# A gated scan and two MLPs on one core: the first products of a slot split by PSUM bank, and their copy in two steps

## The chip, the cores and the metric

The kernel runs on one core of a Trainium2 chip. What is measured is the device time of one execution in microseconds (us). Engines are named as the profile names them: PE is TensorE's matmul, PEld its weight load, DVE VectorE, ACT ScalarE, POOL GpSimd, SP SyncE, whose queue issues the DMAs.

## The reference

Three stages run behind each other on 12160 tokens (2 sequences of 6080) with 256 features, all in float32:

```
sig = 1 / (1 + exp(-f_logit));  f = lower_bound + (1 - lower_bound) * sig
h_t = f_t * h_(t-1) + (1 - f_t) * x_t                    # gated scan over the sequence
y   = relu(h @ w_in1)**2 @ w_out1                        # MLP 0, 256 -> 2048 -> 256
z   = y @ w_in2;  out = where(z > 0, z, exp(min(z, 0)) - 1) @ w_out2   # MLP 1, ELU, 256 -> 2048 -> 256
```

## The kernel before

Tokens are cut into 25 blocks: 256, then 22 of 512, then 384, then 256. Each block goes through MLP 0 (m=0, behind the scan) and MLP 1 (m=1). The hidden width is cut into 8 groups g. One block with one group in one MLP is a *slot* (m, b, g); there are 400. The first four blocks of MLP 0 are "plain" (32 slots); the other 368 slots form their first product from seven smaller products that are combined afterwards, and the change touches these 368 alone. With a block of 512 tokens n is 256, half the block. Blocks are taken in pairs whose slots are woven together, first a pair in MLP 1, then a later pair in MLP 0, and so on: such a *round* of two pairs has 16 slots of m=1 and 16 of m=0, and the middle of the run is a row of equal rounds.

Every float32 number is carried as a high and a low part, so each product is three matmuls. In a slot of the 368:

- `first` (L600 through `products`): 9 matmuls into columns 1, 2 and 3 of a PSUM tile `pc` of four columns of n. A column of 256 float32 is 1 KB, so columns 0 and 1 lie in one 2 KB bank, 2 and 3 in the next. Two `pc` tiles rotate.
- `snap` (L628, ACT): one copy of columns 1 to 3 out to the tile `s`. It is called "the copy" below. `pair` (L631, DVE) adds two of its columns.
- `out` (L699): the second product of an earlier slot, from its `g` tile; 24 matmuls of 256 columns for m=1, 12 of 512 for m=0. In PE's order it mostly lies between `first` and `later`; in some slots near the two ends of the run nothing lies there.
- `later` (L600): 12 matmuls that add to columns 0 to 3 of the same `pc`. They change what the copy has to read before, so they come behind it.
- Then `common` (L636, DVE, reads column 0), `mid_blocks` (L643, DVE, columns 2 and 3), `last_block` (L639, DVE), `first_block` (L646, ACT, column 1), which write the tile `r`; for m=0 `relu` (L649) and `square` (L652) on ACT, for m=1 `below` (L656) and `exp` (L659) on ACT and `elu` (L662) on DVE; and `high_part` (L667, ACT) and `low_part` (L672, DVE), which make `g`.

The order of the work is made when the program is built. `pe_order` fixes PE's order. Every step is given to `Order` with an engine, an assumed duration, a due time and the keys that it reads and writes; `Order.run` plays the engines forward with these assumed numbers, takes on each engine the ready step with the earliest due time, and writes the instructions in the order in which the steps began in that plan. The keys serve the plan alone. Which semaphores an instruction waits for is worked out afterwards from the tiles that the written instructions touch. Each engine runs its instructions strictly in the written order. These lines give the steps that the change touches:

```
"first": ["PE", ... 4.5 * ROW * 2 * n, in_due[s], first, [*X[:2], ws], [pc, ("pe",)]],
"later": ["PE", 6 * ROW * 2 * n, mid_due[s], later, [*X, ws], [pc, ("pe",)]],
["ACT", act(3 * n, True), snap, [pc], [sk]],
["DVE", dve(n), common, [pc, sk], [(*sk, 0), rk]],
["ACT", act(n, True), first_block, [pc, rk], [r0]],
```

Of the kernel before, what the change touches and what calls it, by code (L numbers as in the profile page):

```python
# [15 lines left out]
P = 128  # L16
# [138 lines left out]
def kernel(  # L155
# [59 lines left out]


    NW, NX = 7, 7
    FIRST_PRODUCTS = ((0, 0, 1), (3, 1, 2), (5, 2, 3))
    LATER_PRODUCTS = ((2, 3, 1), (4, 5, 0), (6, 4, 2), (1, 6, 3))
    PLAIN_PRODUCTS = ((1, 0, 0), (3, 1, 0), (0, 0, 1), (2, 1, 1))  # L220

    def plain(m, b):
        return m == 0 and b < PLAIN
# [9 lines left out]
    def new(tag, shape, dtype=F32, name=None):  # L233
        return pools[tag].tile(shape, dtype, tag=name or tag, name=name or tag)
# [29 lines left out]
    for i, s in enumerate(slots + [None] * (LAG + 1)):  # L264
        n = sizes[s[1]] if s else 0
        if s:
            if s[0] == 1 and s[2] == 0:
                while any(p[:2] == (0, s[1]) for _, p, _ in pending):
                    _, p, _ = pending.pop(0)
                    pe_order.append(("out", p))  # L270
                    out_due[p] = now
                    now += 12 * ROW * sizes[p[1]]
            pe_order.append(("first", s))
            in_due[s] = now
            now += (12 if plain(*s[:2]) else 4.5) * ROW * n
        while pending and (not s or i - pending[0][0] >= LAG or now - pending[0][2] >= AGE * sizes[pending[0][1][1]] / TB):
            _, p, _ = pending.pop(0)
            pe_order.append(("out", p))
            out_due[p] = now
            now += 12 * ROW * sizes[p[1]]  # L280
        if s:
            pe_order.append(("later", s))
            mid_due[s] = now
            now += (0 if plain(*s[:2]) else 6) * ROW * n
            pending.append((i, s, now))
# [3 lines left out]
    def act(n, psum=False):  # L289
        return (0.05 if psum else 0.09) + n / 1172  # L290
# [300 lines left out]
    def add_slot(i, m, b, g, wk):  # L591
# [3 lines left out]
        tag = set_of[m, b]  # L595

        def products(which, ws):
            for w, v, c in which:
                for q, (p, r) in enumerate(((0, 0), (0, 1), (1, 0))):
                    nc.tensor.matmul(  # L600
                        t["pc"][:, c], lhsT=ws[:, p, w], rhs=x_t[m, b][:, r, v],
                        start=(which is FIRST_PRODUCTS and q == 0 and c in (1, 2)), stop=(q == 2),
                        skip_group_check=True,
                    )

        def first(e):
            t["pc"] = ph.tile([P, 4, HB], F32, tag="pc", name="pc")[:, :, :n]
            t["ws"] = ws = ws_t[m, g]
            if not plain(m, b):
                products(FIRST_PRODUCTS, ws)  # L610
                return
            for w, k, c in PLAIN_PRODUCTS:
                for q, (p, r) in enumerate(((0, 0), (0, 1), (1, 0))):
                    nc.tensor.matmul(  # L614
                        t["pc"][:, 2 * c : 2 * c + 2], lhsT=ws[:, p, w], rhs=x_t[m, b][:, r, 2 * k : 2 * k + 2],
                        start=(k == 0 and q == 0), stop=(k == 1 and q == 2),
                    )
# [2 lines left out]
            t["r"] = new("r", [P, 4 * HB])[:, : 4 * n]  # L620
            nc.scalar.activation(t["r"].rearrange("p (q i) -> p q i", q=4), t["pc"], AF.Relu)

        def later(e):
            products(LATER_PRODUCTS, t["ws"])

        def snap(e):
            t["s"] = new("s", [P, 3, HB])[:, :, :n]
            nc.scalar.activation(t["s"], t["pc"][:, 1:4], AF.Copy)  # L628

        def pair(e):  # L630
            nc.vector.tensor_tensor(t["s"][:, 1], t["s"][:, 1], t["s"][:, 2], op=ALU.add)  # L631
# [70 lines left out]
        if g == 0:  # L702
# [3 lines left out]
        accs = acc_k[m, b]  # L706
        X = [(*tag, k) for k in range(2 if plain(m, b) else 4)]
        pc, sk, rk, gk = (x + (i,) for x in (("pc",), ("s",), ("r",), ("g",)))
        sk = ("s", n_s[0])
        n_s[0] += not plain(m, b)  # L710
        ek = ("e", n_elu[0])
# [2 lines left out]
        r0, r1, r2, r3, r4 = ((*rk, k) for k in range(5))  # L714
        gh, gl = (*gk, 0), (*gk, 1)
        pe = {
            "first": ["PE", (12 if plain(m, b) else 4.5) * ROW * 2 * n, in_due[s], first, [*X[:2], ws], [pc, ("pe",)]],
            "later": ["PE", 6 * ROW * 2 * n, mid_due[s], later, [*X, ws], [pc, ("pe",)]],
            "out": ["PE", 12 * ROW * 2 * n, out_due[s], out_mm, [gh, gl, ("w", m, g)], [*accs, ("pe",)]],
        }  # L720
        N = 4 * n
        before = [
            ["ACT", act(3 * n, True), snap, [pc], [sk]],
            ["DVE", dve(n), pair, [sk], [(*sk, 1)]],
        ]
        after = [
            ["DVE", dve(n), common, [pc, sk], [(*sk, 0), rk]],
            ["DVE", dve(2 * n), mid_blocks, [pc, (*sk, 0), rk], [r1]],
            ["DVE", dve(n), last_block, [(*sk, 0), (*sk, 1), rk], [r2]],
            ["ACT", act(n, True), first_block, [pc, rk], [r0]],  # L730
        ]
        if plain(m, b):
            before = []
            after = [
                ["ACT", act(N, True), whole_relu, [pc], [rk]],
                ["ACT", act(N), square, [rk], [r4]],
            ]
        elif m == 0:
# [101 lines left out]
    for kind, s in pe_order:  # L840
# [11 lines left out]
        if kind != "later" or not plain(m, b):  # L852
            one = made[s][0][kind]
            order.add(one[0], one[1], one[2], *one[3:])
        if kind == "later":
            chain(out_due[s], made[s][2])
        if kind == "first":
            chain(mid_due[s], made[s][1])
        if kind == "out" and g == KG - 1:
            add_evacuation(m, b)  # L860
# [34 lines left out]
```

## Time and profile before

| | us |
|---|---|
| three runs | 2182.74, 2184.99, 2193.29 (median 2184.99) |
| the profiled execution | 2181.22 |
| its span, first to last instruction | 2179.4 |
| PE busy | 2085.8 (96%) |
| PEld busy | 1968.1 (90%) |
| DVE busy | 1729.9 (79%) |
| ACT busy | 1712.1 (79%) |

Busy time is the union of an engine's instructions, and the rest of the span is idle. An idle stretch is put down to the instruction whose semaphore ended it. The first matmul starts at 25.8 us and the plain slots end near 207 us; from about 410 to 1783 us the rounds follow each other at a pitch of some 172.3 us; behind that come the small last blocks. The granted TensorE clock is 9 tenths or more in each of the 40 slices of the page. In rows of the order, as the built program has it, a wait is shown in square brackets by the engine whose semaphore is waited for, and x11 stands for eleven equal instructions that follow each other.

### The profile page before, as it was taken

What the parts mean: (1) busy time and instruction counts of PE and PEld (TensorE: products, weight loads), DVE (VectorE), ACT (ScalarE), POOL (GpSimd) and SP (SyncE); (2) the same over time, 40 slices, a digit from 0 to 9 for tenths busy, and PEclk for the clock granted to TensorE, in tenths of its full rate; (3) what the DMA queues carried; (4) which work ended last, traced back from release to release, by engine and by line L of the source; (5) the groups of instructions that cost most, each with busy time, mean ns of one, the idle gap of its engine ahead of it and who ended that gap; (6) DMA issues with size and microseconds to landing.
All of it is one profiled execution on the core that took longest, in us unless ns stands there. A gap on an engine that the chain in (4) does not pass through costs nothing.

```text
span 2179.4 us, 38016 instructions
## 1 busy us (share of the span) xinstructions
PE 2085.8 (96%) x15072; PEld 1968.1 (90%) x15072; DVE 1729.9 (79%) x2938; ACT 1712.1 (79%) x2243; POOL 0.2 (0%) x4
## 2 busy tenths in 40 slices
PE   2999899999999999999999999999999999999998
PEld 1877889999999899899899899999999989999998
DVE  5787896986985986987887798798698598677675
ACT  3786787887887887888888888788788788778675
POOL 0000000000000000000000000000000000000000
PEclk9999999999999999999999999999999999999999
DMA  5777643432542442433433433343253243233524
GB/s 154 218 236 241 194 157 108 120 124 94 135 130 95 130 130 92 133 101 119 120 109 124 126 102 124 113 115 126 100 136 122 95 123 127 87 112 106 185 85 141
DMA packets 213049, 282.84 MB, mean 130 GB/s; under 512 B 111112, under 2 KB 137608, under 8 KB 212872
## 3 DMA queue, kind: packets, MB, share of 16 engines
q1 hardware_dynamic: 212872, 280.42, 41.2%
q8 instruction: 119, 1.95, 0.4%
q14 instruction: 58, 0.48, 0.1%
HBM read 236.59 MB, written 43.78 MB: 129 GB/s over the span
## 4 chain that ended last, share of the span: by engine, by line
PE 68%; DVE 19%; ACT 6%; DMA 4%; issue 2%; SPq 1%; DVEq 0%; ACTq 0%
PE acc L699 35%; PE pc L600 31%; DVE g L672 4%; DVE r L643 2%; DVE F L565 2%; PE pc L614 1%; DVE r L662 1%; DVE s L631 1%; ACT s L628 1%; DVE r L639 1%; DMA ws<-wd 1%; DVE s L636 1%; DMA xs<-in_x_dram 1%; DVE fT L548 1%; DVE xA L500 1%
## 5 line engine op out<-in xcount | busy, mean ns | idle before, releaser
L699 PE MATMUL acc<-wo,g 128*128 128x256 f32 x4560 | 585.1, 283 | 17.8 <-DVE g L672 16.7
L699 PEld LDWEIGHTS acc<-wo,g 128*128 128x128 f32 x4560 | 561.3, 189 | 23.2 <-DVE g L672 21.4
L699 PE MATMUL acc<-g,wo 128*128 128x512 f32 (+2 forms) x2400 | 555.9, 382 | 2.1 <-DVE wo L403 2.1
L600 PE MATMUL pc<-xB,ws 128*128 128x256 f32 (+2 forms) x3864 | 507.6, 281 | 11.7 <-ACT s L628 11.2
L600 PE MATMUL pc<-xA,ws 128*128 128x256 f32 (+2 forms) x3864 | 506.3, 280 | 12.9 <-ACT s L628 12.9
L600 PEld LDWEIGHTS pc<-xA,ws 128*128 128x128 f32 x3864 | 481.6, 189 | 24.2 <-ACT s L628 18.5
L672 DVE TENSOR_TENSOR g<-r,g 128x1024 fp32r<-128x1024 f32 (+2 forms) x400 | 465.6, 1164 | 45.0 <-ACT g L667 43.9
L600 PEld LDWEIGHTS pc<-xB,ws 128*128 128x128 f32 x3864 | 482.5, 189 | 20.4 <-ACT s L628 13.7
L699 PEld LDWEIGHTS acc<-g,wo 128*128 128x128 f32 x2400 | 427.8, 189 | 78.0 <-DVE wo L403 2.3
L667 ACT ACTIVATE g<-r 128x1024 fp32r<-128x1024 f32 (+2 forms) x400 | 406.3, 1016 | 58.0 <-DVE r L662 50.6
L636 DVE TENSOR_TENSOR s<-pc,s 128x256 f32<-128x256 f32 (+2 forms) x368 | 150.5, 409 | 286.8 <-PE pc L600 286.1
L628 ACT ACTIVATE s<-pc 128x768 f32<-128x768 f32 (+2 forms) x368 | 286.9, 780 | 62.4 <-PE pc L600 61.1
L643 DVE TENSOR_TENSOR r<-pc,s 128x512 f32<-128x512 f32 (+2 forms) x368 | 244.3, 664 | 11.3 <-ACT r L646 5.9
L662 DVE SCALAR_TENSOR_TENSOR r<-e,r 128x1024 f32<-128x1024 f32 (+1 forms) x200 | 232.3, 1162 | 25.2 <-ACT e L659 25.2
L646 ACT ACTIVATE r<-pc 128x256 f32<-128x256 f32 (+2 forms) x368 | 137.0, 372 | 139.2 <-DVE r L643 87.1
L656 ACT ACTIVATE e<-r 128x1024 f32<-128x1024 f32 (+1 forms) x200 | 202.8, 1014 | 19.3 <-DVE r L639 14.9
L649 ACT ACTIVATE r<-r 128x768 f32<-128x768 f32 (+2 forms) x168 | 138.5, 824 | 97.8 <-DVE r L639 97.7
L652 ACT ACTIVATE r<-r 128x1024 f32<-128x1024 f32 (+1 forms) x200 | 203.6, 1019 | 5.7
L659 ACT ACTIVATE e<-e 128x1024 f32<-128x1024 f32 (+1 forms) x200 | 203.2, 1016 | 5.1
L631 DVE TENSOR_TENSOR s<-s 128x256 f32<-128x256 f32 (+2 forms) x368 | 150.1, 408 | 16.8 <-ACT s L628 9.4
L639 DVE TENSOR_TENSOR r<-s 128x256 f32<-128x256 f32 (+2 forms) x368 | 149.5, 406 | 0.0
L614 PE MATMUL pc<-xA,ws 128*128 128x256 f32 (+1 forms) x192 | 41.0, 368 | 29.0 <-DVE xA L494 25.8
(49 smaller groups left out, 858.0 us busy)
## 6 DMA issues: line engine op xcount, KB each, us to landing
ws<-wd SPq DMA_DIRECT2D x192, 896.0 KB
out_dram<-o SPq DMA_DIRECT2D x47, 256.0 KB
fs<-in_f_logit_dram SPq DMA_DIRECT2D x176, 64.0 KB
xs<-in_x_dram SPq DMA_DIRECT2D x176, 64.0 KB
xd<-o SPq DMA_DIRECT2D x44, 256.0 KB
F<-xd SPq DMA_DIRECT2D x44, 256.0 KB
st<-in_moe_w_out_dram SPq DMA_DIRECT2D x16, 512.0 KB
wd<-wp SPq DMA_DIRECT2D x24, 256.0 KB
```

The costliest lines, as they stand in the source:

```text
L600: nc.tensor.matmul(t["pc"][:, c], lhsT=ws[:, p, w], rhs=x_t[m, b][:, r, v], start=(which is FIRST_PRODUCTS and q == 0 and c in (1, 2)), st ...
L628: nc.scalar.activation(t["s"], t["pc"][:, 1:4], AF.Copy)
L631: nc.vector.tensor_tensor(t["s"][:, 1], t["s"][:, 1], t["s"][:, 2], op=ALU.add)
L636: nc.vector.tensor_tensor(t["s"][:, 0], t["pc"][:, 0], t["s"][:, 0], op=ALU.add)
L643: nc.vector.tensor_tensor(t["c"][:, 1:3], t["pc"][:, 2:4], u, op=ALU.add)
L652: nc.scalar.activation(t["r"], t["r"], AF.Square)
L656: nc.scalar.activation(t["e"], t["r"], AF.Relu, scale=-1.0)
L659: nc.scalar.activation(t["e"], t["e"], AF.Exp, scale=-1.0)
L662: nc.vector.scalar_tensor_tensor(t["r"], t["e"], 1.0, t["r"], op0=ALU.subtract, op1=ALU.max)
L667: nc.scalar.activation(t["g"][:, 0], t["r"], AF.Copy)
L672: nc.vector.tensor_tensor(t["g"][:, 1], t["r"], t["g"][:, 0].bitcast(F32), op=ALU.subtract)
L699: nc.tensor.matmul(a, lhsT=u, rhs=v, start=clear and k == 0, stop=two and k == 2, skip_group_check=True)
```

## The change

The nine matmuls of `first` become two steps: three into column 1 (`first`, one bank) and six into columns 2 and 3 (`next`, the other bank), in the same order as before. The twelve of `later` become six into columns 0 and 1 (`later`) and six into columns 2 and 3 (`last`); here the order of the columns changes from 1, 0, 2, 3 to 0, 1, 2, 3. The copy becomes two copies, column 1 by itself and columns 2 and 3. In the planner's keys `pc` becomes two keys, p0 and p1, one for each bank; `first_block` and `common` now ask for p0 alone. The PSUM tile `pc` is still one tile of two banks. Lines of the changed kernel: products L608, copies L638, `pair` L642, `common` L647, `last_block` L650, `mid_blocks` L654, `first_block` L657, `relu` L660, `square` L663, `below` L667, `exp` L670, `elu` L673, `high_part` L678, `low_part` L683, `out` L710.

```diff
-    FIRST_PRODUCTS = ((0, 0, 1), (3, 1, 2), (5, 2, 3))
-    LATER_PRODUCTS = ((2, 3, 1), (4, 5, 0), (6, 4, 2), (1, 6, 3))
+    PRODUCTS = {
+        "first": ((0, 0, 1),), "next": ((3, 1, 2), (5, 2, 3)),
+        "later": ((4, 5, 0), (2, 3, 1)), "last": ((6, 4, 2), (1, 6, 3)),
+    }
...
             pe_order.append(("first", s))
             in_due[s] = now
             now += (12 if plain(*s[:2]) else 4.5) * ROW * n
+            if not plain(*s[:2]):
+                pe_order.append(("next", s))
...
             pe_order.append(("later", s))
+            if not plain(*s[:2]):
+                pe_order.append(("last", s))
...
-        def snap(e):
-            t["s"] = new("s", [P, 3, HB])[:, :, :n]
-            nc.scalar.activation(t["s"], t["pc"][:, 1:4], AF.Copy)
+        def snap(a, z):
+            def go(e):
+                if a == 1:
+                    t["s"] = new("s", [P, 3, HB])[:, :, :n]
+                nc.scalar.activation(t["s"][:, a - 1 : z - 1], t["pc"][:, a:z], AF.Copy)
+            return go
...
-            "first": ["PE", (12 if plain(m, b) else 4.5) * ROW * 2 * n, in_due[s], first, [*X[:2], ws], [pc, ("pe",)]],
-            "later": ["PE", 6 * ROW * 2 * n, mid_due[s], later, [*X, ws], [pc, ("pe",)]],
+            "first": ["PE", (12 if plain(m, b) else 1.5) * ROW * 2 * n, in_due[s], first, [*X[:2], ws], [p0, ("pe",)]],
+            "next": ["PE", 3 * ROW * 2 * n, in_due[s], more("next"), [*X[:2], ws], [p1, ("pe",)]],
+            "later": ["PE", 3 * ROW * 2 * n, mid_due[s], more("later"), [*X, ws], [p0, ("pe",)]],
+            "last": ["PE", 3 * ROW * 2 * n, mid_due[s], more("last"), [*X, ws], [p1, ("pe",)]],
...
-            ["ACT", act(3 * n, True), snap, [pc], [sk]],
-            ["DVE", dve(n), pair, [sk], [(*sk, 1)]],
+            ["ACT", act(n, True), snap(1, 2), [p0], [(*sk, 0)]],
+            ["ACT", act(2 * n, True), snap(2, 4), [p1, (*sk, 0)], [(*sk, 1)]],
+            ["DVE", dve(n), pair, [(*sk, 1)], [(*sk, 1)]],
...
-            ["DVE", dve(n), common, [pc, sk], [(*sk, 0), rk]],
-            ["DVE", dve(2 * n), mid_blocks, [pc, (*sk, 0), rk], [r1]],
+            ["DVE", dve(n), common, [p0], [(*sk, 0), rk]],
+            ["DVE", dve(2 * n), mid_blocks, [p1, (*sk, 0), rk], [r1]],
             ["DVE", dve(n), last_block, [(*sk, 0), (*sk, 1), rk], [r2]],
-            ["ACT", act(n, True), first_block, [pc, rk], [r0]],
+            ["ACT", act(n, True), first_block, [p0, rk], [r0]],
```

**Place 1: PE, near the end of the run, a slot with nothing between its first nine and its last twelve matmuls (block of 384, n = 192).** Before:

```order
L600 MATMUL pc<-xA,ws 128x192 [waits PE_49]
L600 MATMUL pc<-xA,ws 128x192 x8
L600 MATMUL pc<-xA,ws 128x192 [waits Activation_49]
L600 MATMUL pc<-xA,ws 128x192 x11
L600 MATMUL pc<-xA,ws 128x192 [waits DVE_49,PE_49]
L600 MATMUL pc<-xA,ws 128x192 x8
```

And now:

```order
L608 MATMUL pc<-xA,ws 128x192 [waits PE_49]
L608 MATMUL pc<-xA,ws 128x192 x8
L608 MATMUL pc<-xA,ws 128x192 [waits Activation_49]
L608 MATMUL pc<-xA,ws 128x192 x5
L608 MATMUL pc<-xA,ws 128x192 [waits Activation_49]
L608 MATMUL pc<-xA,ws 128x192 x5
L608 MATMUL pc<-xA,ws 128x192 [waits DVE_49,PE_49]
L608 MATMUL pc<-xA,ws 128x192 x8
```

The twelve matmuls had one wait for ACT, ahead of the first; here they have two, ahead of the first and the seventh. The built program has this second wait in 14 of the 368 slots.

**Place 2: ACT, m=0 slots in the middle of a round (s is the tile of the copy, r<-pc is `first_block`, 768 wide is `relu`, r<-r 1024 `square`, g `high_part`).** Before:

```order
L646 ACTIVATE r<-pc 128x256 [waits DVE_49,PE_49]
L628 ACTIVATE s<-pc 128x768 [waits PE_49]
L649 ACTIVATE r<-r 128x768 [waits DVE_49]
L652 ACTIVATE r<-r 128x1024 [waits Activation_49]
L667 ACTIVATE g<-r 128x1024 [waits Activation_49]
```

And now, two slots:

```order
L657 ACTIVATE r<-pc 128x256 [waits DVE_49]
L638 ACTIVATE s<-pc 128x256 [waits PE_49]
L660 ACTIVATE r<-r 128x768 [waits DVE_49]
L638 ACTIVATE s<-pc 128x512
L663 ACTIVATE r<-r 128x1024 [waits Activation_49]
L678 ACTIVATE g<-r 128x1024 [waits Activation_49]
L638 ACTIVATE s<-pc 128x256 [waits PE_49]
L657 ACTIVATE r<-pc 128x256 [waits DVE_49]
L638 ACTIVATE s<-pc 128x512
L660 ACTIVATE r<-r 128x768 [waits DVE_49]
L663 ACTIVATE r<-r 128x1024 [waits Activation_49]
L678 ACTIVATE g<-r 128x1024 [waits Activation_49]
```

The copy stood in one piece behind `first_block`; its second step now stands behind `relu` in one slot and behind `first_block` in the next, and has no wait of its own.

**Place 3: ACT, the change from m=0 to m=1 within a round.** Before:

```order
L628 ACTIVATE s<-pc 128x768 [waits PE_49]
L646 ACTIVATE r<-pc 128x256 [waits DVE_49]
L492 ACTIVATE xB<-F 128x768 [waits DMAHW2_49]
L537 ACTIVATE fs<-fs 128x512 [waits DMAHW2_49,DMAHW3_49,DMAHW1_49,DMAHW0_49]
L649 ACTIVATE r<-r 128x768 [waits DVE_49]
L652 ACTIVATE r<-r 128x1024 [waits Activation_49]
L667 ACTIVATE g<-r 128x1024 [waits Activation_49]
L628 ACTIVATE s<-pc 128x768 [waits PE_49]
```

And now:

```order
L638 ACTIVATE s<-pc 128x256 [waits PE_49]
L657 ACTIVATE r<-pc 128x256 [waits DVE_49]
L638 ACTIVATE s<-pc 128x512
L660 ACTIVATE r<-r 128x768 [waits DVE_49]
L545 ACTIVATE fs<-fs 128x512 [waits DMAHW6_49,DMAHW7_49,DMAHW5_49,DMAHW4_49]
L663 ACTIVATE r<-r 128x1024 [waits Activation_49]
L500 ACTIVATE xB<-F 128x768
L678 ACTIVATE g<-r 128x1024 [waits Activation_49]
L638 ACTIVATE s<-pc 128x256 [waits PE_49]
```

The first copy here stood whole ahead of `first_block` of the slot before; its second step now stands behind it. Over the whole program the two steps follow each other directly in 99 of the 368 slots; in the others one or more instructions stand between them, mostly `first_block`, `high_part` or `relu`.

## Rows read from the trace of the kernel before

**Rows 1.** The page: span, and busy time of each engine.
```profile
span 2179.4 us, 38016 instructions
PE 2085.8 (96%) x15072; PEld 1968.1 (90%) x15072; DVE 1729.9 (79%) x2938; ACT 1712.1 (79%) x2243; POOL 0.2 (0%) x4
```

**Rows 2.** Waits of PE, whole run: waiter, waited for, us in total, times, longest.
```profile
PE pc L600 <- ACT s L628: 24.1, 27, 2.3
PE acc L699 <- DVE g L672: 16.7, 23, 1.6
```

**Rows 3.** Waits of PE from 410 to 1785 us, the rounds.
```profile
PE acc L699 <- DVE g L672: 13.9, 16, 1.6
PE pc L600 <- ACT s L628: 4.5, 8, 0.7
```

**Rows 4.** Waits of PE from 200 to 410 us.
```profile
PE pc L600 <- ACT s L628: 9.4, 8, 2.3
```

**Rows 5.** Waits of PE from 1785 us to the end.
```profile
PE pc L600 <- ACT s L628: 10.2, 11, 1.9
```

**Rows 6.** Groups by line and shape, ACT reading PSUM: busy us, mean ns.
```profile
L628 ACT ACTIVATE s<-pc 128x768 f32<-128x768 f32 x328 | 264.8, 807 | 48.8 <-PE pc L600 47.8
L646 ACT ACTIVATE r<-pc 128x256 f32<-128x256 f32 x328 | 125.1, 382 | 112.8 <-DVE r L643 74.4 <-DVE s L636 37.8
L779 ACT ACTIVATE o<-acc 128x512 f32<-128x512 f32 x47 | 26.3, 583 | 2.4 <-PE acc L699 2.3
```

**Rows 7.** Timeline of PE, a late slot with nothing between: start, us, what.
```profile
2105.89 1.24 PE L600 MATMUL pc<-xB,ws 128*128 128x256 f32 x9
2108.03 1.68 PE L600 MATMUL pc<-xB,ws 128*128 128x256 f32 x12 [0.90 <-ACT s L628]
```

**Rows 8.** Timeline of ACT, the same slot.
```profile
2107.17 0.81 ACT L628 ACTIVATE s<-pc 128x768 f32<-128x768 f32 x1 [0.35 <-PE pc L600]
```

**Rows 9.** Timeline of ACT, m=0 in the middle of a round.
```profile
1190.32 0.38 ACT L646 ACTIVATE r<-pc 128x256 f32<-128x256 f32 x1 [0.26 <-DVE r L643]
1190.60 0.81 ACT L628 ACTIVATE s<-pc 128x768 f32<-128x768 f32 x1
1192.24 0.85 ACT L649 ACTIVATE r<-r 128x768 f32<-128x768 f32 x1 [0.83 <-DVE r L639]
1193.12 1.06 ACT L652 ACTIVATE r<-r 128x1024 f32<-128x1024 f32 x1
1194.22 1.06 ACT L667 ACTIVATE g<-r 128x1024 fp32r<-128x1024 f32 x1
```

**Rows 10.** Timeline of DVE, the same slot.
```profile
1189.08 0.42 DVE L636 TENSOR_TENSOR s<-pc,s 128x256 f32<-128x256 f32 x1 [2.09 <-PE pc L600]
1189.54 0.69 DVE L643 TENSOR_TENSOR r<-pc,s 128x512 f32<-128x512 f32 x1
1190.15 1.22 DVE L672 TENSOR_TENSOR g<-r,g 128x1024 fp32r<-128x1024 f32 x1
1191.79 0.42 DVE L639 TENSOR_TENSOR r<-s 128x256 f32<-128x256 f32 x1
```

**Rows 11.** Timeline of PE, the last twelve of that slot and of the next.
```profile
1192.68 1.57 PE L600 MATMUL pc<-xA,ws 128*128 128x256 f32 x12
1197.90 1.57 PE L600 MATMUL pc<-xB,ws 128*128 128x256 f32 x12
```

**Rows 12.** Timeline of ACT, the change from m=0 to m=1.
```profile
1072.88 0.38 ACT L646 ACTIVATE r<-pc 128x256 f32<-128x256 f32 x1 [1.10 <-DVE r L643]
...
1082.74 1.06 ACT L667 ACTIVATE g<-r 128x1024 fp32r<-128x1024 f32 x1 [0.69 <-DVE r L662]
```

**Rows 13.** Timeline of PE, the same stretch.
```profile
1072.54 2.63 PE L600 MATMUL pc<-xA,ws 128*128 128x256 f32 x21
...
1078.46 2.74 PE L600 MATMUL pc<-xA,ws 128*128 128x256 f32 x21 [0.54 <-ACT s L628]
...
1083.78 1.45 PE L600 MATMUL pc<-xA,ws 128*128 128x256 f32 x11
```

More of the change, by code (lines that the diff above doesn't have):

```diff
@@ L597, in products @@
         def products(which, ws):
-            for w, v, c in which:
+            for w, v, c in PRODUCTS[which]:
                 for q, (p, r) in enumerate(((0, 0), (0, 1), (1, 0))):
@@ L601, in products @@
                         t["pc"][:, c], lhsT=ws[:, p, w], rhs=x_t[m, b][:, r, v],
-                        start=(which is FIRST_PRODUCTS and q == 0 and c in (1, 2)), stop=(q == 2),
+                        start=(which in ("first", "next") and q == 0 and c in (1, 2)), stop=(q == 2),
                         skip_group_check=True,
@@ L609, in first @@
             if not plain(m, b):
-                products(FIRST_PRODUCTS, ws)
+                products("first", ws)
                 return
@@ L621, in whole_relu, with more @@
             nc.scalar.activation(t["r"].rearrange("p (q i) -> p q i", q=4), t["pc"], AF.Relu)
-        def later(e):
-            products(LATER_PRODUCTS, t["ws"])
-        def snap(e):
-            t["s"] = new("s", [P, 3, HB])[:, :, :n]
-            nc.scalar.activation(t["s"], t["pc"][:, 1:4], AF.Copy)
+        def more(which):
+            return lambda e: products(which, t["ws"])
+        def snap(a, z):
[4 more added lines that the diff above has]
+            return go
         def pair(e):
@@ L708, in add_slot @@
         pc, sk, rk, gk = (x + (i,) for x in (("pc",), ("s",), ("r",), ("g",)))
+        p0, p1 = (*pc, 0), (*pc, 1)
         sk = ("s", n_s[0])
@@ L734, in add_slot @@
             after = [
-                ["ACT", act(N, True), whole_relu, [pc], [rk]],
+                ["ACT", act(N, True), whole_relu, [p0], [rk]],
                 ["ACT", act(N), square, [rk], [r4]],
@@ L854 @@
             order.add(one[0], one[1], one[2], *one[3:])
-        if kind == "later":
+        if kind == ("later" if plain(m, b) else "last"):
             chain(out_due[s], made[s][2])
-        if kind == "first":
+        if kind == ("first" if plain(m, b) else "next"):
             chain(mid_due[s], made[s][1])
```

## The prediction

> **What bounds the kernel now.** I read the page first: PE is busy 2085.8 of a span of 2179.4 us, DVE and ACT 79% each [rows 1]. So PE sets the time, and only work that takes or gives back PE's idle time counts. The waits of PE come next. For the copy (ACT s L628) PE waited 24.1 us in 27 pieces, and for `g` 16.7 us in 23 [rows 2]. By stretch: eight of the copy's waits, 9.4 us, lie before 410 us [rows 4], eight, 4.5 us, in the rounds [rows 3], eleven, 10.2 us, behind them [rows 5]. A copy can be waited for at most 24.1 us, which is 1.1% of the run, and that is all that a better copy could give. In a round, PE's idle time is one wait for the copy of about 0.56 us and two for `g`, 13.9 / 8 = 1.74 us together [rows 3]: 2.3 us of a pitch of 172.3.
>
> In the middle of a round the copy is covered. PE's m=0 pitch is 1197.90 - 1192.68 = 5.22 us [rows 11], and the copy ends at 1190.60 + 0.81 = 1191.41 [rows 9], 1.27 us before PE's twelve at 1192.68 need it. Where nothing lies between the nine and the twelve, the copy is bare: it runs 2107.17 to 2107.98 [rows 8] and PE starts at 2108.03 after 0.90 us of idling [rows 7], which is the copy's 0.81 and 0.09 for the two hand-overs.
>
> **What the built order says of the split.** The idea needs two things: the first copy must start after three matmuls, and the six matmuls on the first bank must start after the first copy. The built program has neither. In all 368 slots the first copy waits for the ninth matmul, not the third: when it is written, `next` has been written already, and both touch the tile `pc`. In 354 slots the second copy has no wait of its own, and the twelve matmuls have none at the seventh: the wait at their first is for the second copy. `common`, which reads column 0 alone, still waits for the twenty-first matmul in all 368. In the remaining 14 slots (place 1) the plan puts the second copy behind `later`; there the second copy waits for the fifteenth matmul and the sixteenth for the second copy, so PE waits twice. Waits go by the tile, and the two keys live in the plan alone. Nothing becomes earlier; what is left is the cost of a second instruction and of the new order.
>
> **Part by part.**
>
> Matmuls: 21 before and after, of the same sizes; the other order of columns costs nothing that I can name, and the trace has no row in which two orders differ. I bound it at 0 on both sides, since PE's twelve take 1.57 us in every steady slot [rows 11] whichever weights they use.
>
> The second instruction. ACT reads 256 columns of PSUM in 0.382 us, 512 in 0.583 and 768 in 0.807 [rows 6]; an independent instruction starts 0.10 us before the one ahead ends (1190.60 against 1190.32 + 0.38) [rows 9]. Two steps side by side take 0.382 + 0.583 - 0.10 = 0.865, so +0.06 us; apart, up to +0.16. Over 368 slots ACT works 22 to 59 us more in its 467 idle us. On PE's path this counts only where PE already waits for the copy and waits once: 27 - 14 = 13 waits, 13 x 0.06 = **+0.8 us**.
>
> The 14 double waits. Before, such a slot loses 0.90 [rows 7]. Now: 0.38 + 0.09 for the first copy, six matmuls, 0.58 + 0.09 for the second: 1.14, so +0.24 if ACT stands ready. In 11 of the 14 one or more other instructions stand between the two steps, 0.38 to over 1 us long; six matmuls (0.8 us) cover most of such a one. The bounds are +0.24 and +0.24 + 0.5 a slot, 3.4 to 10 us; I take 0.36, the nearer to the row: **+5.0 us**.
>
> The m=0 loop (place 2). The second copy now stands behind `relu` of the slot before, or behind its `first_block`, and both hang on DVE. I follow the chain through two slots, with the durations of [rows 6, 9, 10], +0.03 to 0.04 us for each hand-over and -0.10 where two instructions of one engine overlap: `relu` 0.85, `square` 1.09, `high_part` 1.09, `first_block` 0.28, `mid_blocks` 0.73, `relu` 0.89, second copy 0.49, `square` 0.96, `high_part` 1.09, `low_part` 1.26 (it now stands ahead of the next `common`), `common` 0.34, `mid_blocks` 0.73, `first_block` 0.42, second copy 0.49, and back to `relu`, which overlaps by 0.10. The sum is 10.61 us, while PE's two slots take 10.44. The 1.27 us of cover is thus used up and PE falls back by some 0.17 in two slots. About five pairs of slots in a round run this way, less the slack left at the start: I take +0.5 a round, between 0 (one hand-over less than I count) and 1.5. There are nine such stretches: **+4.5 us**. In m=1 `out` is longer, and the second copy behind `high_part` still keeps about 0.6 us by the same count, so nothing there.
>
> The change from m=0 to m=1 (place 3), nine times. The second copy stands behind the `first_block` that ran at 1072.88 [rows 12]: it would end at 1072.88 + 0.38 + 0.58 - 0.10 = 1073.74, and PE needed it at 1072.54 [rows 13]: a new wait of 1.25. The next slot's wait of 0.54 [rows 13] stays about as it is. In the slot behind it the second copy stands behind the `high_part` that ended at 1083.80 [rows 12], so it ends at about 1084.3 against 1083.78 [rows 13]: between 0 (if PE has fallen back by then) and 0.6. Against this, when PE comes later, the 1.74 us for `g` shrink, by up to 1.4. Net -0.2 to +1.9; I take +0.9: **+8 us**.
>
> Here a rule of the skill bears. PE's waits for the copy are bubbles that an engine with 467 idle us causes [rows 1, 2]. The Trainium skill, "Perfetto Trace Analysis", section "Optimizing Scalar/DVE Operations", says that where ScalarE or VectorE is not saturated but causes bubbles elsewhere, breaking instructions up may let work be completed sooner. That rule speaks for the change, and no run here shows it yet; by it the sum would be the first rival's.
>
> Sum: 0.8 + 5.0 + 4.5 + 8 = 18.3 us on the profiled execution's 2181.2, so 2199.5. The median of the runs shown lies 3.8 above that execution; I split the difference and forecast **2202 us**.
>
> **Rivals.**
>
> *The split works by bank.* Then the twelve matmuls need only the first copy, 0.38 instead of 0.81, and each of the 27 waits gives back 0.43: 11.6 us, or 2173 on the median, faster. That rule of the Trainium skill is the case for it. It decides where the wait at the tenth matmul is for the first copy; the built program has that only in the 14 slots with a second wait behind. A luckier order could still shorten the `g` waits, which only the trace can show. Chance 0.09.
>
> *Nothing visible.* The second copy's 0.06 us hides in 1.27 us of cover, the loop is one hand-over shorter than I count and never binds, and at the change of MLP the later PE saves in `g` waits what it loses for the copy. What is left is the double waits and the 0.8 us: 5 or 6 us, 2188 to 2190. For it: the loop's excess, 0.17 of 10.44 us, is smaller than the error of its hand-overs. Against it: the 1.25 us at place 3 is a sum of four numbers, and only a `first_block` that runs earlier than at 1072.88 takes it away. Chance 0.26.
>
> *The loop binds from the start of each m=0 stretch.* If each of the loop's four hand-overs between ACT and DVE costs 0.09 (what the bare copy pays for its two) instead of 0.04, the loop is 10.81 us and PE loses 0.37 in two slots, 2.6 us in seven pairs, 23 us in nine rounds, and with the other terms 37: 2220. Chance 0.10.
>
> **How the numbers follow.** The forecast, slower by 8 to 28 us, has 0.55; its own range is 2192 to 2214. Nothing visible has 0.26, the binding loop 0.10, the bank split and better luck 0.09. About 0.5%, 11 us, is about what a measurement of this kernel can tell from no change. Faster by more than that needs the first rival whole: 0.08. Within it lie the second rival, a little of the first and the lower end of the forecast: 0.28. Slower: 0.64. For 8 in 10 the range leaves out most of the bank split below and the upper part of the binding loop: 2183 to 2222.
>
> **What would show it.** ACT should have 2611 instructions, 368 more, and its busy time should be 22 to 59 us higher; PE's busy time and PE's count of 15072 should stay. PE's wait for the copy should rise from 24.1 us to about 40, with new pieces at the seventh of the twelve in 14 slots, about 1 us at each change from m=0 to m=1, and short ones in the m=0 stretches; the wait for `g` should not rise much. In a bare slot the first copy should start behind the ninth matmul. I am wrong if the first copy starts behind the third, if PE's copy waits fall, or if the round's pitch stays at 172.3 us or goes below it.

## The result, and the profile after

The changed kernel takes 2207.3 us (median of 4 runs, 2205.7 to 2212.1), the kernel before 2183.9 (4 runs) on the same chip: 1.0105 times as long, with a 95% interval of 1.0076 to 1.0133. So it is slower by about 1%. The profiled execution took 2207.83 us, 26.6 more than that of before. Its page:

```profile
span 2205.8 us, 38214 instructions
...
PE 2105.4 (95%) x15072; PEld 1976.0 (90%) x15072; DVE 1735.6 (79%) x2933; ACT 1726.7 (78%) x2616; POOL 0.2 (0%) x4
```

Beside [rows 1] the span grew by 26.4 us. Only 6.8 of that is idle time of PE (2205.8 - 2105.4 = 100.4, against 93.6); the other 19.6 stands as busy time of PE, though the matmuls are the same 15072; the filling experiments below come back to that. The waits of PE in the whole run (waiter, waited for, us in total, times, longest), which answer to [rows 2]:

```profile
PE pc L608 <- ACT s L638: 34.7, 52, 1.9
...
PE acc L710 <- DVE g L683: 10.8, 14, 1.3
```

The copy is waited for 52 times instead of 27, 10.6 us more; `g` costs 5.9 us less. By stretch, first 200 to 410 us, which answers to [rows 4]:

```profile
PE pc L608 <- ACT s L638: 11.7, 14, 1.9
```

then the rounds, 410 to 1800 us, against [rows 3]:

```profile
PE acc L710 <- DVE g L683: 9.2, 8, 1.3
PE pc L608 <- ACT s L638: 8.6, 15, 0.8
```

and the end, from 1800 us, against [rows 5]:

```profile
PE pc L608 <- ACT s L638: 14.4, 23, 1.0
```

In the rounds the two waits together stay as they were (17.8 us, 18.4 before). The start of one slot's first matmul in both traces, subtracted, says where the time is lost: after lags by -0.8 us at slot 0 (the first of the 368), +11.2 at slot 40, +15.6 at slot 296, +26.4 at the end. So 12.0 us are lost in the first 40 slots, 4.4 in the eight rounds, 10.8 behind them.

The 4.4 us of the rounds are lost although PE is hardly longer idle there (0.1 us more from slot 40 to slot 296). The starts of the matmuls show where, with the usual distance between two starts taken as the median for their shape: behind each idle stretch the next matmul starts some 0.16 us later than the stretch is long, since the recorded ends are modelled and overlap the next start, and the rounds have 36 such stretches instead of 24 (1.9 us more); 46 starts instead of 26 come late with no idle time shown at all (2.2 us more).

The slot of [rows 7, 8], where nothing lies between the nine matmuls and the twelve. Timeline of PE (start, us, what, idle time before it and its releaser):

```profile
2107.20 1.26 PE L608 MATMUL pc<-xB,ws 128*128 128x256 f32 x9
2108.93 0.97 PE L608 MATMUL pc<-xB,ws 128*128 128x256 f32 x6 [0.47 <-ACT s L638]
2110.59 0.98 PE L608 MATMUL pc<-xB,ws 128*128 128x256 f32 x6 [0.69 <-ACT s L638]
```

Timeline of ACT in the same slot:

```profile
2108.49 0.38 ACT L638 ACTIVATE s<-pc 128x256 f32<-128x256 f32 x1 [0.37 <-PE pc L608]
2108.77 0.84 ACT L667 ACTIVATE e<-r 128x768 f32<-128x768 f32 x1
2109.94 0.60 ACT L638 ACTIVATE s<-pc 128x512 f32<-128x512 f32 x1 [0.33 <-PE pc L608]
```

The first copy starts behind the ninth matmul (2107.20 + 1.26 = 2108.46), not the third; six matmuls follow it, the second copy waits for these, and six more follow that. One wait of 0.90 has become 0.47 + 0.69.

ACT's groups of copies by shape (busy us, mean ns, then idle time before and its releaser), against [rows 6]:

```profile
L638 ACT ACTIVATE s<-pc 128x512 f32<-128x512 f32 x328 | 194.6, 593 | 4.2 <-PE pc L608 3.9
L638 ACT ACTIVATE s<-pc 128x256 f32<-128x256 f32 x352 | 134.1, 381 | 72.2 <-PE pc L608 70.7
```

593 + 381 = 974 ns for what took 807. (The 352 of the second line hold 24 second copies of the small blocks besides the 328 first copies.) ACT's busy time rose by 14.6 us. The new plan also moved five steps that may run on either engine from DVE (2938 to 2933 instructions) to ACT.

### The profile page after: what moved, and what is told of

It reads as the page before. It is cut to its first block, busy times and chain, and to the rows that moved or that the text cites. A ratio compares the mean times of both kernels' runs of the same rounds, so it can differ in the third digit from the quotient of the medians.

```text
span 2205.8 us, 38214 instructions
## 1 busy us (share of the span) xinstructions
PE 2105.4 (95%) x15072; PEld 1976.0 (90%) x15072; DVE 1735.6 (79%) x2933; ACT 1726.7 (78%) x2616; POOL 0.2 (0%) x4
## 4 chain that ended last, share of the span: by engine, by line
PE 68%; DVE 19%; ACT 6%; DMA 4%; issue 2%; SPq 1%; DVEq 0%; ACTq 0%
PE acc L710 36%; PE pc L608 31%; DVE g L683 4%; DVE F L573 2%; DVE r L654 2%; DVE r L673 2%; DMA st<-in_moe_w_in_dram 2%; PE pc L622 1%; DMA fs<-in_f_logit_dram 1%; ACT g L678 1%; DVE r L650 1%; DVE s L642 1%; DVE s L647 1%; ACT s L638 1%; SPq L541 1%
## 5 line engine op out<-in xcount | busy, mean ns | idle before, releaser
L710 PE MATMUL acc<-wo,g 128*128 128x256 f32 x4560 | 588.8, 284 | 11.8 <-DVE g L683 10.6
L710 PEld LDWEIGHTS acc<-wo,g 128*128 128x128 f32 x4560 | 565.2, 190 | 17.2 <-DVE g L683 15.2
L710 PE MATMUL acc<-g,wo 128*128 128x512 f32 (+2 forms) x2400 | 559.9, 383 | 3.2 <-DVE wo L411 3.0
L683 DVE TENSOR_TENSOR g<-r,g 128x1024 fp32r<-128x1024 f32 (+2 forms) x400 | 466.3, 1166 | 114.8 <-ACT g L678 114.0
L608 PE MATMUL pc<-xA,ws 128*128 128x256 f32 (+2 forms) x3864 | 512.9, 282 | 21.0 <-ACT s L638 20.6
L608 PE MATMUL pc<-xB,ws 128*128 128x256 f32 (+2 forms) x3864 | 512.0, 281 | 15.0 <-ACT s L638 14.1
L608 PEld LDWEIGHTS pc<-xA,ws 128*128 128x128 f32 x3864 | 484.3, 190 | 38.3 <-ACT s L638 33.2
L608 PEld LDWEIGHTS pc<-xB,ws 128*128 128x128 f32 x3864 | 482.9, 189 | 29.4 <-ACT s L638 23.9
L710 PEld LDWEIGHTS acc<-g,wo 128*128 128x128 f32 x2400 | 431.3, 191 | 79.9 <-DVE wo L411 3.4
L678 ACT ACTIVATE g<-r 128x1024 fp32r<-128x1024 f32 (+2 forms) x400 | 406.9, 1018 | 91.7 <-DVE r L673 81.0
L638 ACT ACTIVATE s<-pc 128x256 f32<-128x256 f32 (+2 forms) x736 | 338.1, 473 | 98.7 <-PE pc L608 96.3
L647 DVE TENSOR_TENSOR s<-pc,s 128x256 f32<-128x256 f32 (+2 forms) x368 | 150.6, 409 | 216.5 <-PE pc L608 216.4
L654 DVE TENSOR_TENSOR r<-pc,s 128x512 f32<-128x512 f32 (+2 forms) x368 | 244.2, 664 | 16.9 <-ACT r L657 13.5
L657 ACT ACTIVATE r<-pc 128x256 f32<-128x256 f32 (+2 forms) x368 | 136.9, 372 | 135.4 <-DVE s L647 80.9
L673 DVE SCALAR_TENSOR_TENSOR r<-e,r 128x1024 f32<-128x1024 f32 (+1 forms) x200 | 232.3, 1161 | 7.0 <-ACT e L670 6.8
L667 ACT ACTIVATE e<-r 128x1024 f32<-128x1024 f32 (+1 forms) x200 | 202.3, 1011 | 17.6 <-DVE r L650 16.8
L670 ACT ACTIVATE e<-e 128x1024 f32<-128x1024 f32 (+1 forms) x200 | 203.0, 1015 | 4.1
L663 ACT ACTIVATE r<-r 128x1024 f32<-128x1024 f32 (+1 forms) x200 | 203.1, 1016 | 3.8
L642 DVE TENSOR_TENSOR s<-s 128x256 f32<-128x256 f32 (+2 forms) x368 | 150.5, 409 | 45.8 <-ACT s L638 45.3
L660 ACT ACTIVATE r<-r 128x768 f32<-128x768 f32 (+2 forms) x168 | 138.6, 825 | 45.6 <-DVE r L650 32.8
L650 DVE TENSOR_TENSOR r<-s 128x256 f32<-128x256 f32 (+2 forms) x368 | 150.2, 408 | 3.9
```

The source lines that it names most:

```text
L608: nc.tensor.matmul(t["pc"][:, c], lhsT=ws[:, p, w], rhs=x_t[m, b][:, r, v], start=(which in ("first", "next") and q == 0 and c in (1, 2)), ...
L638: nc.scalar.activation(t["s"][:, a - 1 : z - 1], t["pc"][:, a:z], AF.Copy)
L647: nc.vector.tensor_tensor(t["s"][:, 0], t["pc"][:, 0], t["s"][:, 0], op=ALU.add)
L654: nc.vector.tensor_tensor(t["c"][:, 1:3], t["pc"][:, 2:4], u, op=ALU.add)
L663: nc.scalar.activation(t["r"], t["r"], AF.Square)
L667: nc.scalar.activation(t["e"], t["r"], AF.Relu, scale=-1.0)
```

## The experiments

Each was timed in three rounds beside the kernel before on the same chip; its median there was 2183.6 to 2185.1 us. Ratios are to that kernel, with 95% intervals. "Slot 40" and "slot 296" bound the eight rounds, as above; "lag" is against the trace of before.

**One copy again, the rest as changed** (e1_one_copy).

```diff
-            ["ACT", act(n, True), snap(1, 2), [p0], [(*sk, 0)]],
-            ["ACT", act(2 * n, True), snap(2, 4), [p1, (*sk, 0)], [(*sk, 1)]],
+            ["ACT", act(3 * n, True), snap(1, 4), [p0, p1], [(*sk, 0), (*sk, 1)]],
```

> The changed kernel with one copy of columns 1 to 3 again; the matmuls in four steps and the plan's two keys stay. Against the kernel before (2183.9), the changed one takes 2207.3. Theory of the copies (the second instruction and the places it stands in cost the time): 2184 to 2189, PE's wait for the copy near 24 us, no wait at the seventh of the twelve, each round back at 172.3 us, granted clock about 0.997. Rival, the plan's keys (common and first_block are planned for the end of the first bank, which the built waits do not give them): most stays, 2196 to 2206, rounds at 172.8 us.

Measured: 2201.8 us, 1.0069 [1.0044, 1.0095], within the rival's range and above the theory's. Its interval overlaps that of the change; at best it gives back part. Its waits in the rounds:

```profile
PE acc L710 <- DVE g L683: 5.4, 16, 0.4
PE pc L608 <- ACT s L638: 2.8, 9, 0.3
```

Here the rounds are better than before (8.2 us of waits against 18.4; the lag falls from 8.0 to 2.8 us), and all the loss lies at the two ends, 8 us up to slot 40 and 14.5 behind slot 296. So in this plan the split copy costs the rounds about 9.6 us (4.4 + 5.2 of lag), and something other than the second instruction makes the ends slow.

**Both copies in one step of the plan** (e2_copies_together).

```diff
+        def both(e):
+            snap(1, 2)(e)
+            snap(2, 4)(e)
...
+            ["ACT", act(n, True) + act(2 * n, True), both, [p0, p1], [(*sk, 0), (*sk, 1)]],
```

> The changed kernel with the two copies written as one step of the plan, so they always follow each other directly and no wait at the seventh of the twelve arises. Theory of the copies' places: the second instruction alone costs 0.06 us at some 27 waits, 1.6 us, and the time is 2185 to 2190. Rival, the second instruction itself: 22 us of ACT time that pushes everything behind it, 2200 or more. Rival, the plan's keys: as the kernel with one copy, whatever that gives.

Measured: 2212.2 us, 1.0108 [1.0074, 1.0143], as the rival of the second instruction had it; PE's wait for the copy is 41.1 us. In the total, side by side is no better than apart. The stretches differ, though: the lag is 4.9 us at slot 40, 6.7 at slot 296 and 30.0 at the end, so the head and the rounds lose less than in the change and the end loses more, where this execution's TensorE clock stood at its lower level for 38 us (14 in the change; the filling experiments below come back to the clock). Beside the kernel with one copy, whose lag falls by 5.2 us over the rounds where this one's rises by 1.8, the second instruction costs 7 us in the rounds.

**The PSUM tile cut into two tiles of one bank** (e3_two_tiles). The copies, `common`, `mid_blocks` and `first_block` read the tile that holds their columns, and the plain slots' `relu` becomes two instructions; plan and order are the change's.

```diff
-            t["pc"] = ph.tile([P, 4, HB], F32, tag="pc", name="pc")[:, :, :n]
+            t["pc"] = [ph.tile([P, 2, HB], F32, tag=f"p{k}", name=f"p{k}")[:, :, :n] for k in range(2)]
...
-                        t["pc"][:, c], lhsT=ws[:, p, w], rhs=x_t[m, b][:, r, v],
+                        t["pc"][c // 2][:, c % 2], lhsT=ws[:, p, w], rhs=x_t[m, b][:, r, v],
```

> The changed kernel with the PSUM tile of four columns cut into two tiles of one bank each (plain slots then read it in two steps), so that the waits go by bank: in the built program the first copy waits for the third matmul, the ten-th matmul for the first copy, the sixteenth for the second copy, common for the fifteenth. Theory that the waits by tile void the split: a bare slot's wait of 0.90 or 1.14 us goes to about nothing (the first copy runs under the six matmuls of the second bank, the second copy under the six of later), the copy's waits fall from 34.7 to under 10 us, granted clock back near 0.997, and the time is 2160 to 2178, faster than before. Rival, the places of the second copy decide: in the rounds it stands behind the same instructions, the rounds keep 172.8 us, and the time is 2190 to 2200.

Measured: **2159.2 us, 0.9869 [0.9838, 0.9901]**, faster than both kernels and just under the theory's range. Its page:

```profile
span 2156.9 us, 38314 instructions
...
PE 2081.3 (96%) x15072; PEld 1967.5 (91%) x15072; DVE 1726.6 (80%) x2933; ACT 1737.8 (81%) x2648; POOL 0.2 (0%) x4
```

Its waits of PE:

```profile
PE acc L711 <- DVE g L684: 14.6, 21, 1.2
PE p L608 <- ACT s L639: 7.9, 13, 1.3
```

The copy is waited for 7.9 us instead of 34.7. A bare slot again, on PE:

```profile
2065.84 2.00 PE L608 MATMUL p<-xB,ws 128*128 128x256 f32 x15
2068.08 0.98 PE L608 MATMUL p<-xB,ws 128*128 128x256 f32 x6 [0.25 <-ACT s L639]
```

and on ACT:

```profile
2066.42 0.39 ACT L639 ACTIVATE s<-p 128x256 f32<-128x256 f32 x1 [0.33 <-PE p L608]
2066.70 0.84 ACT L668 ACTIVATE e<-r 128x768 f32<-128x768 f32 x1
2067.44 0.59 ACT L639 ACTIVATE s<-p 128x512 f32<-128x512 f32 x1
```

The first copy now runs beside `next` (it starts 0.58 us behind the first matmul), so the nine and the first six of the twelve run as one piece of 15; what is left is 0.25 us for the second copy, which stands behind `below`. The lag is -2.9 us at slot 40, -11.0 at slot 296 and -22.6 at the end. The plan is the same, so what decides between 2207 and 2159 is the tile that the waits go by (the relu in two instructions belongs to the 32 plain slots alone, which lie ahead of slot 0).

**No second wait: the plan may not put the second copy behind `later`** (e4_no_second_wait).

```diff
-            "later": ["PE", 3 * ROW * 2 * n, mid_due[s], more("later"), [*X, ws], [p0, ("pe",)]],
+            "later": ["PE", 3 * ROW * 2 * n, mid_due[s], more("later"), [*X, ws], [p0, p1, ("pe",)]],
```

> The changed kernel with one edit: the plan's step later asks for both banks, so that the second copy is always written ahead of it. The 14 second waits go; copies stay apart elsewhere. Theory that the two waits cost what their rows say (0.47 + 0.69 in place of 0.90): 14 x 0.25 = 3.5 us less, 2203 to 2205, clock as in the changed kernel (0.988). Rival, the granted clock: the second waits are what lets PE's clock fall to half in 200 to 275 us and 2050 to 2085 us; then these stretches come back to full clock, 10 us or more less, 2193 to 2197, clock 0.995 or more.

Measured: 2209.9 us, 1.0105 [1.0073, 1.0136], above both expected ranges. The double waits are gone, and nothing is won:

```profile
PE pc L608 <- ACT s L638: 40.2, 40, 2.4
```

Twelve waits fewer than after, but longer ones, 5.5 us more in all. This execution also stood at half clock for longer, 43 us against 32; what is lost apart from the clock hardly changes (by the matmuls' starts, 0.9 us less in the first 40 slots and 0.5 less behind the rounds). So taking the double waits away moves the loss into single waits and does not remove it.

**The plan with one key for both banks** (e6_one_key), so that it plans with the waits that the program really has.

```diff
-        p0, p1 = (*pc, 0), (*pc, 1)
+        p0 = p1 = (*pc, 0)
```

> The changed kernel with one edit: the plan's two keys are one and the same, so the plan knows that both copies come behind the nine matmuls, that later comes behind both copies, and common behind the twelve; the two copies follow each other directly in 211 slots (99 in the changed kernel) and no second wait arises. Theory that the plan's false keys place the instructions badly: rounds at 172.3 us, time 2185 to 2192 apart from the clock. Rival, the second instruction itself (two copies together cost 7 us more over the rounds than one copy): 2195 to 2205.

Measured: 2195.3 us, 1.0040 [1.0023, 1.0056]. About 12 us of the change's 23.4 come from the plan counting on waits by bank; 11 remain with the two copies. The lag is 2.0 us at slot 40, 1.5 at slot 296, 13.6 at the end: the rounds and the head are repaired, the tail is not, and most of what the tail loses goes with the clock: 24 us at half clock behind slot 296, against 3 in before.

**The kernel before with the new order of columns alone** (x1_column_order).

```diff
-    LATER_PRODUCTS = ((2, 3, 1), (4, 5, 0), (6, 4, 2), (1, 6, 3))
+    LATER_PRODUCTS = ((4, 5, 0), (2, 3, 1), (6, 4, 2), (1, 6, 3))
```

> The kernel before, with one edit: the twelve matmuls go through the columns in the order 0, 1, 2, 3 in place of 1, 0, 2, 3. Nothing else moves. Theory that the order of columns costs nothing: 2183 to 2188, the same waits and clock as before. Rival, it is what lowers the clock in all variants: 2192 or more.

Measured: 2185.8 us, 1.0017 [1.0000, 1.0035]. The interval alone leaves room for 0.35%, 7.6 us. The trace is narrower: PE's busy time is 2085.6 us against 2085.8, and the eight rounds, in which the clock does not fall in any of the traces, take 1378.7 us against 1378.8. So the order of columns costs nothing that shows.

**Filling PE's gaps.** In PE's 19.6 us of additional busy time the granted clock has a part. The page does not show it, since a slice of 55 us averages it out; a timeline of PE in a late stretch of after does:

```profile
2052.91 2.45 PE L608 MATMUL pc<-xA,ws 128*128 128x128 f32 x21
2056.00 4.54 PE L608 MATMUL pc<-xA,ws 128*128 128x128 f32 x21 [0.64 <-ACT s L638]
2060.34 2.87 PE L710 MATMUL acc<-g,wo 128*128 128x256 f32 x12
```

The same work in before:

```profile
2037.81 2.45 PE L600 MATMUL pc<-xA,ws 128*128 128x128 f32 x21
2040.85 2.56 PE L600 MATMUL pc<-xA,ws 128*128 128x128 f32 x21 [0.59 <-ACT s L628]
2043.25 1.64 PE L699 MATMUL acc<-g,wo 128*128 128x256 f32 x12
```

The 21 matmuls take 4.54 us instead of 2.56, and the 12 behind them 2.87 instead of 1.64: 3.2 us lost that no wait shows. Windows of after over that stretch (start:end, length, busy time of PE, PEld, DVE, ACT, POOL with counts, granted clock, DMA share, GB/s):

```profile
2050.00:2055.00 5.00, 5.00 (x47) 5.00 (x45) 1.88 (x6) 2.78 (x7) 0.00 (x0) 1.00 0.73 247
2055.00:2060.00 5.00, 4.36 (x24) 4.22 (x22) 2.17 (x7) 1.59 (x4) 0.00 (x0) 0.63 0.59 190
2060.00:2065.00 5.00, 5.00 (x33) 5.00 (x33) 1.33 (x4) 2.91 (x7) 0.00 (x0) 0.69 0.54 181
2065.00:2070.00 5.00, 4.03 (x35) 3.83 (x35) 2.40 (x7) 2.28 (x6) 0.00 (x0) 0.99 0.57 184
```

The granted clock has two levels, 2.4 and 1.2 GHz; 0.63 of 5 us means that 3.7 of them ran at the lower one. Summed over windows of 10 us from 60 us on, PE stood at the lower level for 32 us in after and 15 in before, none of it in the rounds. If at half clock half the work is done (the 12 matmuls above took 2.87 us where 1.64 were usual), the difference, 17 us, is worth about 8.7 us: an estimate from these windows. Counted from slot 0 to the last matmul, the stretch over which the lag is read, it is 31 us against 7, worth about 12. To test the clock's part, six matmuls with zero weights, which add nothing to an open accumulator, were put ahead of `later` in the 13 bare slots that have an accumulator open, so that PE works where it would wait for the copy. If idle time were all that is lost there, they could not gain anything. First in the changed kernel (f1_after_fill):

```diff
+    zero = const.tile([P, P], F32R, name="zero")
...
+        def fill():
+            if plain(m, b) or t["outs"] != n_out[0] or not n_out[1] or n_out[1][2] == KG - 1:
+                return
+            a = acc_t[n_out[1][:2]][0][:, :n]
+            for _ in range(6):
+                nc.tensor.matmul(a, lhsT=zero, rhs=x_t[m, b][:, 0, 0], start=False, stop=False, skip_group_check=True)
...
+                if which == "later":
+                    fill()
```

> The changed kernel, with six matmuls of zero weights added (they add 0 to an open accumulator) between the nine and the twelve of 13 slots in which nothing lies there and PE waits for the copy. They add 78 matmuls of work and take nothing away. Theory of the clock: in the two stretches with such slots (200 to 430 us and behind 1870 us) the changed kernel's PE ran some 32 us at half clock, because PE idled there; with PE kept busy the half-clock time falls to 15 us or less and the time to 2195 to 2203, although PE does more. Rival, the waits themselves cost the time: 2205 to 2210, clock as in the changed kernel or not.

Measured: 2199.6 us, 1.0070 [1.0047, 1.0093]: more matmuls, and 7.7 us less, though the two intervals overlap; 24 us at half clock instead of 32, where 15 or less were expected.

Then with the single copy (e1 with the same filling, f2_one_copy_fill):

> The same filling in the kernel with one copy, which took 2201.8 with 45 us at half clock and 8 us less idling in the rounds than the kernel before. Theory of the clock: 2182 to 2193, and its runs, which lay between 2192.5 and 2212.7, come closer together. Rival, the waits: 2199 to 2205.

Measured: 2188.3 us, 1.0020 [1.0007, 1.0032], 13.5 us less than without it; 11 us at half clock instead of 45. Its ten runs lie within 8.3 us, those without the filling within 20.2.

In the kernel before (f4_before_fill):

> The kernel before with the same filling (six matmuls of zero weights in each of the 13 slots). Theory of the clock: the filling works through the clock, and the kernel before has 15 us at half clock, most of it not at these slots, so there is little to win: 2178 to 2185. Rival, the filling shortens waits or helps in some other way than by the clock: a gain as in the changed kernel, 7 us or more, 2177 or less.

Measured: 2180.2 us, 0.9986 [0.9976, 0.9997], 3.4 us less.

In the kernel whose plan has one key (f6_one_key_fill):

> The filling in the kernel whose plan has one key (2195.3, 37 us at half clock, 1.5 us lost in the rounds). Theory of the clock: 2183 to 2190, so that what is left against the kernel before is the second instruction and its places. Rival: 2193 to 2197.

Measured: 2186.0 us, 1.0004 [0.9989, 1.0019], 9.3 us less.

In the kernel with two tiles (f3_two_tiles_fill):

> The filling in the kernel with two tiles of one bank each (2159.2, 14 us at half clock, hardly a wait left in these slots). Theory of the clock: nothing to win, and 13 x 0.6 us of matmuls that no wait covers any more: 2160 to 2167, slower than without. Rival, the filling helps whatever the waits: 2150 to 2156.

Measured: 2161.5 us, 0.9902 [0.9887, 0.9918], 2.3 us more, which the intervals do not tell from nothing. Where PE hardly waits in the bare slots, the filling has nothing to win.

The two largest gains have intervals that lie apart. Whether they come by the clock, the stretches of the traces can tell (one execution of each kernel): in the rounds, where the clock never falls, the filling changes at most 0.3 us, and at the two ends its gain goes with the time at half clock that it takes away.

| kernel | slots 0 to 40: us gained, us less at half clock | from slot 296 on: us gained, us less at half clock |
|---|---|---|
| after | 3.0, 6.8 | 4.8, 10.2 |
| one copy | 6.3, 17.1 | 6.5, 13.7 |
| one key | 1.1, 3.4 | 9.4, 20.5 |
| before | 1.5, 3.4 | 0.0, 0.0 |
| two tiles | 1.4, 3.4 | -3.2, 0.0 |

Each gain is between a third and a half of the time beside it, near the half of the estimate, but for the two tiles behind slot 296, where there was no half clock to take away and the additional matmuls went with 3.2 us more. With the filling on both sides, after minus before is 2199.6 - 2180.2 = 19.4 us, the one copy 8.1, the one key 5.8.

The timed executions give the clock's part once more. The kernel before took 2178.9 to 2181.0 us in the seven executions whose mean granted clock was 0.993, and 2192.6 to 2194.0 in the four at 0.985 or 0.986. At 0.988 it took 2189.1 and 2190.5, the changed kernel 2206.8 and 2207.8: at an equal clock about 17 of the 23.4 us remain.

## Why the prediction was right, and where its sum was not

*The built order* held, and with it the result. The prediction said that waits go by the tile, that the first copy starts behind the ninth matmul, and that nothing becomes earlier. The bare slot of after shows it, and the two tiles show the other half: once the tile is what the plan's keys say, the first rival comes true, at 2159 instead of the 2173 worked out for it. That rival was priced too low. It let each of the 27 waits shrink by the difference of two copies, 0.43 us, or 11.6 in all; but with two tiles the first copy runs beside `next`, and of the bare slot's 0.90 us only 0.25 is left. The profiled executions differ by 22.5 us, 18.0 of PE's idle time and 4.5 of its busy time. The rule that spoke for the change (the Trainium skill, "Perfetto Trace Analysis", section "Optimizing Scalar/DVE Operations": breaking up instructions of an unsaturated ScalarE or VectorE may let work complete sooner) thus fails in the changed kernel and holds in the one with two tiles.

*The 14 double waits* were worked out as 0.38 + 0.09 and 0.58 + 0.09; the timeline has 0.47 and 0.69. In the bare slots of the tail each raised the lag by 0.31 to 0.56 us, where 0.36 was taken: about the right size, a little low. Yet without them nothing is won, as the fourth experiment showed.

*The second instruction* was under-estimated. Its term was 0.8 us, on the ground that it counts only where PE already waits for the copy. Even side by side, between the kernels of the first and the second experiment, it costs 7 us in the rounds, though PE waits for the copy there only 9 times in the first of them. Against it stands something else that the sum lacks: with the one copy the new steps and keys give the rounds 5.2 us back.

*The m=0 loop* was over-estimated. The second copy does stand behind `relu` or `first_block` and creeps towards PE. Timeline of ACT in the middle of a round:

```profile
1210.13 0.85 ACT L660 ACTIVATE r<-r 128x768 f32<-128x768 f32 x1 [0.28 <-DVE r L654]
1210.88 0.58 ACT L638 ACTIVATE s<-pc 128x512 f32<-128x512 f32 x1
...
1215.85 0.38 ACT L657 ACTIVATE r<-pc 128x256 f32<-128x256 f32 x1 [0.79 <-DVE r L654]
1216.13 0.59 ACT L638 ACTIVATE s<-pc 128x512 f32<-128x512 f32 x1
```

Timeline of PE there:

```profile
1212.01 1.57 PE L608 MATMUL pc<-xB,ws 128*128 128x256 f32 x12
...
1217.23 0.98 PE L608 MATMUL pc<-xA,ws 128*128 128x256 f32 x7
```

The copy ends at 1211.46 and 1216.72, and PE comes at 1212.01 and 1217.23: 0.55 and 0.51 us are left of the 1.27 of [rows 9, 11]. Over slots 149 to 156 the slack goes 0.67, 0.62, 0.55, 0.50, 0.43, 0.38, 0.32, 0.27. That is 0.12 us for two slots where 0.17 was worked out, and the stretch ends before it is used up. (The sum took 0.03 to 0.04 us for every hand-over; [rows 9, 10] have one of 0.09, from `mid_blocks`, which ends at 1190.23, to `first_block` at 1190.32. With it the loop would be 0.10 us longer, and the measured one is 0.05 us shorter.) Only the last slot of m=0 is touched. ACT and PE there:

```profile
1069.94 0.60 ACT L638 ACTIVATE s<-pc 128x512 f32<-128x512 f32 x1
...
1070.59 2.76 PE L608 MATMUL pc<-xB,ws 128*128 128x256 f32 x21
```

The copy ends at 1070.54 and PE starts at 1070.59; there the lag rises by 0.31 us a round. Predicted was +0.5.

*The change from m=0 to m=1* was over-estimated most. PE there, answering to [rows 13]:

```profile
1087.22 2.77 PE L608 MATMUL pc<-xA,ws 128*128 128x256 f32 x21 [0.69 <-ACT s L638]
...
1092.55 2.63 PE L608 MATMUL pc<-xA,ws 128*128 128x256 f32 x21
...
1098.29 1.68 PE L608 MATMUL pc<-xA,ws 128*128 128x256 f32 x12 [0.36 <-ACT s L638]
```

and ACT, answering to [rows 12]:

```profile
1086.29 0.38 ACT L657 ACTIVATE r<-pc 128x256 f32<-128x256 f32 x1 [0.43 <-DVE r L654]
1086.57 0.59 ACT L638 ACTIVATE s<-pc 128x512 f32<-128x512 f32 x1
...
1096.69 1.06 ACT L678 ACTIVATE g<-r 128x1024 fp32r<-128x1024 f32 x1 [1.09 <-DVE r L673]
1097.65 0.58 ACT L638 ACTIVATE s<-pc 128x512 f32<-128x512 f32 x1
```

The new wait is 0.69 us, not 1.25. Without it PE would have started at 1086.53, 13.99 later than in before; `first_block` started at 1086.29, only 13.41 later than its 1072.88. It stood 0.58 us earlier against PE, which is the case that the second rival named. The wait that was to stay is gone, and the one behind `high_part` is 0.36, within its 0 to 0.6. One wait for `g` has gone as well. The waits of this round are 2.17 us (0.69, 0.36 and 1.12 for `g`) where before had 2.14 (0.54, 0.61, 0.99). Around this place the lag rises by 0.24 us, not 0.9. So the pitch of a round rose by 4.4 / 8 = 0.55 us where the two terms together said 1.4: rightly slower than 172.3, by less than half of what was said.

*The ends* were under-estimated: the sum had 0.8 + 5.0 us for them, and they lost 22.8 (12.0 and 10.8). This is the step that was mis-sized, and two things were missing in it. The plan counts on waits by bank, which the program does not have, and so puts ACT's steps in an order that does not fit the real waits; with the true waits (one key) the lag at slot 40 is 2.0 instead of 11.2. And PE's clock fell there, which the prediction had no term for. Over-estimated rounds (12.5 for 4.4) and under-estimated ends cancelled: the sum, 18.3, stands beside 26.6 between the two profiled executions (23.4 between the medians), and that it came so near is in part luck.

*What would show it*: PE's wait for the copy was to rise to about 40 us (34.7), `g` not to rise (it fell by 5.9). PE's busy time was to stay, and rose by 19.6 us: this is where the sum had no term, for the clock and for the delays that are longer than the idle time shown. ACT was to have 2611 instructions (2616) and 22 to 59 us more busy time (14.6, below the lower end). Summed by instruction the full slots' copies do take (593 + 381 - 807) x 328 = 54.8 us more, but busy time is the union, and the shorter copies overlap more of their neighbours than was counted.

The starts of the matmuls divide what the ends lose. Of the 12.0 us of the first 40 slots, 1.7 are more idle time, 6.2 lie in stretches at half clock (17.1 us of them against 3.4), and 4.0 are, as in the rounds, starts that come later than the idle time shown. Of the 10.8 us behind slot 296, 3.6 are idle time, 4.7 lie at half clock (13.7 us against 3.4) and 2.5 are late starts. The usual distances are medians, so these are estimates from the two traces.

What stays open is what makes the clock fall: ahead of the slow 21 matmuls PE had waited 0.64 us, and ahead of the same ones in before, which kept the full clock, 0.59. Nor is it settled why the kernel with one key loses so much time to the clock behind the rounds.

## What to carry to other kernels

Before splitting a tile's producer and consumer, look in the built order at what the waits go by: keys of a planner do not split a tile, and a plan with finer keys than the waits is worse than one with coarse keys (2207 against 2195 us). Cut the tile itself along the bank, and the same plan wins 1.3%. Where PE waits in short pieces, look at the granted clock of that stretch before adding up the waits alone.

## What was not expected of the hardware

A short wait for the copy was followed by some 7 us at half clock (2056 to 2063 us), in a stretch where PE was busy nearly all the time, and it cost 3.2 us where the wait itself was 0.64. Matmuls that do nothing useful, put into such waits, went with 7.7 to 13.5 us less in three kernels. Also a wait's printed length understates its price: in both traces, in the head, the rounds and the tail, an idle stretch of PE delayed the next start by some 0.16 us more than its length, and at the last m=0 slot PE shows a gap of 36 ns where the lag rises by 0.31 us a round.
